# Gated attention plus feed-forward: when a native P V step may be begun in two halves

## The chip, the cores and the metric

The kernel runs on one core of one Trainium2 chip. The metric is the device time of one execution in microseconds (us). The kernel before was timed three times: 1029.58, 1030.44 and 1033.46 us, median 1030.44 us. The profile shown below is of one more execution.

## The reference, cut to what matters

Multi-query attention (32 heads of 16, one shared key and value head) and a feed-forward block with SiLU work on the same 2048 x 512 input; a sigmoid gate per row mixes their outputs.

```python
q = (x @ wq) in 32 heads of 16; k = x @ wk; v = x @ wv      # x: 2048 x 512
p = softmax(einsum("bhqd,bkd->bhqk", q, k) * 16 ** -0.5)
a = einsum("bhqk,bkd->bhqd", p, v) in 512 columns @ wo
b = silu(x @ w1) @ w2                                       # 512 -> 1792 -> 512
g = sigmoid((x * gate_w).sum(-1))
out = g * a + (1 - g) * b
```

## The kernel before, in words

**Work.** The queries are four chunks of 512 rows; the heads are taken eight at a time. So there are 16 rounds (chunk c, head group o). A round goes over the 2048 keys in 32 steps of 64 keys: 512 steps. A step has two halves j, each with four heads, and each half is one *score* on TensorE (PE; `scores(p)`, line 1225, eight matmuls into one of two `S` banks in PSUM) and one *exponential* on ScalarE (ACT; `exponential(p)`, line 1231). So p, the number of a score and of its exponential, runs from 0 to 1023, and step s has p = 2s and 2s + 1. A score of p needs the bank that exponential p - 2 has left. Both exponentials of a step write one buffer `P` (128 x 2048 float32). There are four such buffers (P_575 to P_578 in the order of instructions), and three more come when three chunks of the input are no longer needed (from about p = 280 on; they lie in the tile `xs`). Exponential 2s needs a buffer that no earlier step still uses.

**P V.** Each step's probabilities are then multiplied by the values (line 1262; `pv`), in one of two manners that the planner picks step by step. *In parts*: VectorE (DVE) takes the difference of P and its upper half as a float16 tile `L` (line 1237, two instructions a step; `L` buffers and two tiles `raw`), and PE makes a pass A on the upper halves and a pass B on `L`. *Native*: PE multiplies the float32 P itself, no DVE work. A native step is done whole (kind "W", eight matmuls of 512 columns, sixteen records in the trace) or, with `HALVES`, in two halves (kind "NM": N on the first 256 columns of each head, M on the others, eight matmuls of 256 columns each); other work may stand between N and M. P is released after M, W, or after A and both `L`.

**Feed-forward, projections.** Their matmuls (line 851) are cut into *passes* of eight matmuls. They are the filler: the planner puts them where PE has nothing more pressing. The hidden units go through a tanh on ACT (line 906) and two DVE instructions.

**Ends of rounds.** The accumulators `pv0`, `pv1` of a round are read by DVE (line 1151, two transposes) before the next round's first P V may start. So at the start of a round the exponentials run ahead into the free P buffers.

**Order.** All of this is ordered when the program is built, by a planner that lets a clock run for each of PE, ACT and DVE and takes for each engine the next piece of work (`advance`, `pe_next`, `act_next`, `dve_next`). On the chip each engine works down its list in that order, and waits where a result that it needs is not there. `pe_next` gathers candidates (ready time, price, kind): a score (price 0), P V (price 1 where the buffers are about to run out or the end is near, 3 for a step in parts or one already begun, 4 for a new native step), a pass (2 while the passes are behind their quota, else 5; 4.5 at the end of a round). Of those ready within 0.03 us of PE's clock it takes the cheapest, else the one that is ready first. `pv_next` offers a native step whole if it ends before the next score is due by the plan. Where it would not, but a half would, it offers "NM":

```python
fits = most if s not in left_of else most + HALF
if HALVES and r is not None and s not in left_of and max(r, now["PE"]) > most:
    fits, kind = most + HALF, "NM"
```

Of the kernel before, what the change touches and what calls it, by code (L numbers as in the profile page):

```python
# [33 lines left out]
BOW = 40 / 2.0 ** 18  # L34

DUE = 2.5
HALVES = True
PAIRS = 3
XUSE = "PPP "
GROUPS = (4, 3, 4, 3), (4, 3, 4, 3), (4, 3, 4, 3), (4, 4, 4, 2)  # L40
# [16 lines left out]
def kernel(  # L57
# [30 lines left out]
    x = x.rearrange("b s d -> (b s) d")  # L88
# [720 lines left out]
    def attention(ctx, pO, scale_of, t_scale, shifts, split_pieces, chores, q_todo, early, gates_, v_bank):  # L809
# [652 lines left out]
        exp_done, mm_done, how, left_of, low_done, pv_done, pv_free = {}, {}, {}, {}, {}, {}, {0: 0.0}  # L1462
# [57 lines left out]
        def pv_next(most):  # L1520

            best = None
            for s in range(head[0], min(head[0] + n_bufs[0], n_exp[0] // 2)):
                i, k = steps[s]
                if i != steps[head[0]][0] or k == NK - 1 and s != head[0]:
                    break
                r = pv_ready(s)
                ab = s in left_of and left_of[s] and left_of[s][0] in "AB"
# [3 lines that stand above are left out]
                else:  # L1532
                    kind = "W"
                if r is not None and (ab or max(r, now["PE"]) <= fits):
                    p = 1 if n_exp[0] - 2 * s >= 2 * n_bufs[0] + LAG - 8 or n_exp[0] >= 2 * len(steps) - SOON else 3 if ab else 4
                    new = (max(r, now["PE"] + 0.03), p, r, s, kind)
                    best = min(best or new, new)
                if s == head[0] and k == 0 and (s not in left_of or left_of[s] == list(how[s])):
                    break
            return best  # L1540
# [35 lines left out]
        def pe_next():  # L1576

            t, p = now["PE"], n_mm[0]
            cands = []
            if p < 2 * len(steps) and (p < 2 or p - 2 in exp_done) and placed[0] > steps[p // 2][1] * 64 // 512:  # L1580
                cands.append((exp_done[p - 2] if p > 1 else START, 0, "S", None))
            q = n_exp[0]
            end = max(now["ACT"], mm_done.get(q, 0.0)) + (p - q) * EXP
            x = pv_next(end - PASS_S - LATE - 2 * HALF + SLACK if p < 2 * len(steps) else 1e9)
            if x:
                cands.append((x[2], x[1], "P", x[3:]))
            if begin_:
                r = begin_[0][0]()
                if r is not None:
                    cands.append((r, begin_[0][1](), "R", None))  # L1590
            else:
                r = work.ready()
                if r is not None:
                    near = head[0] < len(steps) and steps[head[0]][1] >= NK - 2 and 0 < work.n - work.i <= KEEP
                    cands.append((r, 4.5 if near else 2 if work.passes < QUOTA * p + 3 * KD * len(early) - 30 - BOW * p * (2 * len(steps) - p) else 5, "F", None))
            ok = [x for x in cands if x[0] <= t + 0.03]
            return min(ok, key=lambda x: x[1]) if ok else min(cands, key=lambda x: x[0], default=None)

        def act_next():
# [60 lines left out]
        def on_dve(t, n):  # L1660
# [5 lines left out]
            return length  # L1666

        engines = {"PE": (pe_next, on_pe), "ACT": (act_next, on_act), "DVE": (dve_next, on_dve)}

        def advance():  # L1670
# [94 lines left out]
```

## Time and profile before

| | |
|---|---|
| median of three runs | 1030.44 us (1029.58 to 1033.46) |
| the profiled execution's own time | 1030.14 us |
| its span, first to last instruction | 1028.4 us |
| exponentials on ACT | 1024, the first begins at 25.7 us, the last at 1014.6 us |
| tanh instructions on ACT | 56 |
| busy shares on the page | PE 98%, ACT 96%, DVE 90% |
| P V steps before (of 512) | 245 in parts, 130 native whole, 131 native in halves, 6 at the end by code of their own |

The trace gives every instruction its engine, start and length. Two things have to be kept in mind. A matmul's record is longer than the time that it holds PE, since matmuls run into one another: what a piece of work costs on PE is read from its start to the start of what follows. And the record of an exponential is longer than the distance to the next one, so a small delay between two exponentials leaves no idle time in a view of waits; it too is read from start to start. In the time line, rows of one kind are merged: "x5" are five instructions.

### The profile page before, as it was taken

To read this page: it belongs to the slowest core of one execution; us is meant where nothing else is said; L and a number is where in the kernel's file an instruction comes from. 1 tells how busy PE (TensorE), PEld (TensorE's weight loads), DVE (VectorE), ACT (ScalarE), POOL (GpSimd) and SP (SyncE) were. 2 spreads that over 40 slices of the span, in tenths; PEclk is the share of its full clock that TensorE was granted. 3 is DMA by queue.
4 is the path that set the end of the run, shared out by engine and by line. 5 is a ranking of instruction groups with operands and counts; after the bars stand their busy time and mean duration, and the time that the engine had idled before them with its cause. 6 is when DMAs were issued, how large, how long until landed. Compare 5 with 4: busy or idle time off the path is not lost.

```text
span 1028.4 us, 69785 instructions
## 1 busy us (share of the span) xinstructions
PE 1006.5 (98%) x32760; PEld 616.2 (60%) x32760; DVE 924.5 (90%) x1199; ACT 992.3 (96%) x1108; POOL 60.0 (6%) x138
## 2 busy tenths in 40 slices
PE   8999999999999999999999999999999999999996
PEld 6456565666655656565656556566666556565563
DVE  7888978989999999999999999899998989999893
ACT  5999999999999999999999999999999999999994
POOL 4101101100000000000000000000000000000000
PEclk9999999999999999999999999999999999999999
DMA  5123322311010111101011010100110110101001
GB/s 208 48 87 85 82 59 60 76 45 25 10 42 18 48 33 25 30 5 32 19 24 41 24 46 15 35 20 15 47 27 17 43 39 10 36 10 19 5 4 47
DMA packets 28115, 40.14 MB, mean 39 GB/s; under 512 B 5689, under 2 KB 19370, under 8 KB 27818
## 3 DMA queue, kind: packets, MB, share of 16 engines
q0 software_dynamic: 10656, 15.73, 7.4%
q1 hardware_dynamic: 16442, 19.27, 5.9%
q8 instruction: 258, 4.23, 1.8%
q10 hardware_dynamic: 720, 0.59, 0.2%
q14 instruction: 39, 0.32, 0.1%
HBM read 19.98 MB, written 8.25 MB: 27 GB/s over the span
## 4 chain that ended last, share of the span: by engine, by line
PE 83%; ACT 10%; DVE 3%; issue 3%; DMA 1%; SPq 0%; ACTq 0%
PE pm L851 32%; PE pv L1262 28%; PE S L1225 20%; ACT P L1231 7%; ACT xs L1231 2%; DVE L L1237 1%; ACT e L906 1%; PE pv L1250 1%; DMA xn<-in_A_x_dram 1%; PE pt L339 0%; DVE xs L132 0%; DVE e L909 0%; PE pv L518 0%; PE pm L436 0%; PE S L1218 0%
## 5 line engine op out<-in xcount | busy, mean ns | idle before, releaser
L1231 ACT ACTIVATE P<-S 128x1024 f32<-128x1024 f32 x770 | 737.5, 1077 | 10.5 <-PE S L1225 5.5
L1225 PE MATMUL S<-qb,KT 50*32 50x512 f16 x8096 | 483.4, 379 | 5.7 <-ACT P L1231 1.8
L1225 PEld LDWEIGHTS <-KT 50*32 50x32 f16 x8096 | 206.1, 90 | 189.1 <-issue 100.0
L1237 DVE TENSOR_TENSOR L<-P 128x1024 f16<-128x1024 f32 x227 | 271.5, 1217 | 20.7 <-ACT P L1231 19.6
L851 PE MATMUL pm<-xs,w1s 64*32 64x512 f16 x5376 | 274.8, 375 | 1.1 <-DVE e L909 0.8
L851 PE MATMUL pm<-w2s,H 64*32 64x512 f16 x5376 | 273.8, 375 | 1.3 <-DVE e L909 0.8
L1262 PE MATMUL pv<-P,VF 64*32 64x256 f32 (+1 forms) x5056 | 267.5, 450 | 0.3
L1231 ACT ACTIVATE xs<-S 128x1024 f32<-128x1024 f32 x254 | 253.6, 1080 | 2.1 <-PE S L1225 0.9
L851 PEld LDWEIGHTS <-w1s 64*32 64x32 f16 x5376 | 126.5, 93 | 44.2 <-issue 8.4
L851 PEld LDWEIGHTS <-H 64*32 64x32 f16 x5376 | 125.3, 93 | 44.0 <-issue 4.3
L1237 DVE TENSOR_TENSOR raw<-P 128x1024 f16<-128x1024 f32 x109 | 131.1, 1218 | 2.3 <-ACT P L1231 2.0
L1262 PEld LDWEIGHTS pv<-P,VF 64*32 64x32 f32 x5056 | 112.1, 106 | 34.3 <-issue 3.3
L1237 DVE TENSOR_TENSOR L<-xs 128x1024 f16<-128x1024 f32 x90 | 108.0, 1218 | 3.9 <-ACT xs L1231 3.4
L1262 PEld LDWEIGHTS <-VP 64*32 64x32 f16 x3920 | 79.5, 92 | 36.0 <-issue 5.5
L851 PE MATMUL pm<-xs,wqs 64*32 64x512 f16 x1440 | 100.3, 375 | 0.1
L1262 PE MATMUL pv<-L,VP 64*32 64x512 f16 x1268 | 92.3, 375 | 0.3 <-DVE L L1237 0.2
L1262 PE MATMUL pv<-P,VP 64*32 64x512 bf16 x1344 | 81.9, 387 | 0.0
L1237 DVE TENSOR_TENSOR raw<-xs 128x1024 f16<-128x1024 f32 x64 | 76.9, 1217 | 2.4 <-ACT xs L1231 2.2
L851 PE MATMUL pm<-wo_s,O 64*32 64x512 f16 x1440 | 75.1, 375 | 0.6 <-issue 0.2
L918 POOL DMA_DIRECT2D H<-e x56 | 30.4, 542 | 729.4 <-DVE e L909 725.2
L1262 PE MATMUL pv<-xs,VF 64*32 64x256 f32 (+1 forms) x1216 | 62.5, 432 | 0.2 <-issue 0.2
L1262 PE MATMUL pv<-raw,VP 64*32 64x512 f16 x692 | 58.3, 375 | 0.0
(215 smaller groups left out, 710.5 us busy)
## 6 DMA issues: line engine op xcount, KB each, us to landing
H<-e POOLq DMA_DIRECT2D x56, 128.0 KB, 2.5
raw<-in_B_w_dram POOLq DMA_DIRECT2D x24, 256.0 KB, 3.3
qb<-qd SPq DMA_DIRECT2D x180, 32.0 KB
xn<-in_A_x_dram SPq DMA_DIRECT2D x8, 512.0 KB
out_dram<-acc SPq DMA_DIRECT2D x14, 256.0 KB
qd<-qx SPq DMA_DIRECT2D x13, 256.0 KB
raw<-in_A_wo_dram POOLq DMA_DIRECT2D x4, 256.0 KB, 3.1
qb<-sh SPq DMA_DIRECT2D x60, 2.0 KB
```

Source lines behind the costliest of these rows:

```text
L851: nc.tensor.matmul(self.bank[32 * m:32 * m + 32], l(i, rows, 32 * m), r(j, rows), start=first, stop=last)
L906: nc.scalar.activation(e, o.bank, AF.Tanh, scale=t_scale)
L918: nc.gpsimd.dma_start(H[:, 0], e)
L1225: nc.tensor.matmul(sc[32 * m:32 * m + 32, f], KT[b:b + 50, k0:k0 + 32], qtile[i][b:b + 50, m // 2, j], start=True, stop=True)
L1231: nc.scalar.activation(probs[s][:, 2 * j:2 * j + 2], banks.pop(p), AF.Exp, scale=scale_of(*rounds[steps[s][0]]))
L1237: nc.vector.tensor_tensor(lows[s, j], probs[s][:, js], upper(probs[s])[:, js], op=OP.subtract)
L1250: nc.tensor.matmul(pvs[i][h][32 * j:32 * j + 32, 256 * q:256 * q + 256], VF[r, NK - 2 * PAIRS + 2 * u + a], probs[s][r, j, 256 * a:256 * a ...
L1262: nc.tensor.matmul(pvs[i][h][32 * j:32 * j + 32, q], a[r], b[r, q], start=k == 0 and n != "B", stop=k == NK - 1 and n in "BMW")
```

## The change

Where `pe_next` has a new native step on offer that would be begun in halves, it now looks at the other candidates. P V has one candidate at a time, so these are the score and the pass (and the pieces of the beginning). If one of them is ready before PE's clock plus 0.2 us, the step in halves is struck from the list at that moment. It is offered again at the next decision, whole if it then fits. A half M of a step that has been begun is not held back, and price 1 makes no exception. The flag `HALVES` stays true; nothing is changed in what any instruction does.

```diff
-HALVES = True
+HALVES, GAP = True, 0.2
...
             ok = [x for x in cands if x[0] <= t + 0.03]
+            new = [x for x in ok if x[2] == "P" and x[3][1] == "NM" and x[3][0] not in left_of]
+            if new and min((x[0] for x in cands if x not in new), default=1e9) < t + GAP:
+                ok = [x for x in ok if x not in new]
+                cands = [x for x in cands if x not in new]
             return min(ok, key=lambda x: x[1]) if ok else min(cands, key=lambda x: x[0], default=None)
```

Every decision after the first one that differs is made from another state, so the order is dealt anew from there to the end. The counts of the first and only executed pass over the data, from the order of instructions: 244 steps in parts (245 before), 186 native whole (130), 76 native in halves (131). Scores, exponentials, passes and the last six steps are the same in number.

Three places on PE follow, where the prediction speaks of the order. `S_...` is a score, `pv0...<-P_...,VF` with 32x512 a native step done whole, with 32x256 a half of one, `<-P_...,VP` pass A and `<-L...,VP` pass B of a step in parts. "..." leaves out the rest of a piece's eight matmuls, their weight loads and the passes of line 851.

The first place, scores 30 to 32 of round 0, is where the two orders part. Before, the step in P_575 is begun in halves just ahead of score 30:

```order
L1262 MATMUL pv0_791<-P_575,VF_63 32x256
...
L1225 MATMUL S_1359<-qb0_83,KT_60 32x512
...
L1262 MATMUL pv1_792<-P_575,VF_63 32x256
...
L1225 MATMUL S_1377<-qb0_83,KT_60 32x512
...
L1262 MATMUL pv0_791<-P_576,VF_63 32x512
...
L1225 MATMUL S_1399<-qb0_83,KT_60 32x512
```

Now:

```order
L1225 MATMUL S_1348<-qb0_83,KT_60 32x512
...
L1262 MATMUL pv0_791<-P_575,VF_63 32x512
...
L1225 MATMUL S_1369<-qb0_83,KT_60 32x512
...
L1262 MATMUL pv0_791<-P_576,VF_63 32x256
...
L1225 MATMUL S_1400<-qb0_83,KT_60 32x512
```

The half ahead of score 30 is gone, the step in P_575 follows that score whole, and the next native step, whole before, is now the one in halves (its other half comes after score 33).

The second place is the start of round 2: exponential 136 is the first that needs a buffer back from this round. Before, the last P V of round 1 (`pv0_2593`) is the half behind score 132, and the first of round 2 (`pv0_4688`) stands ahead of score 137:

```order
L1262 MATMUL pv0_2593<-P_575,VF_63 32x256
...
L1225 MATMUL S_4559<-qb0_83,KT_60 32x512
...
L1262 MATMUL pv1_2594<-P_575,VF_63 32x256
...
L1225 MATMUL S_4677<-qb0_83,KT_60 32x512
...
L1262 MATMUL pv0_4688<-P_578,VF_63 32x512
...
L1225 MATMUL S_4700<-qb0_83,KT_60 32x512
```

Now (`pv0_4643` is round 2):

```order
L1225 MATMUL S_4527<-qb0_83,KT_60 32x512
...
L1225 MATMUL S_4561<-qb0_83,KT_60 32x512
...
L1262 MATMUL pv0_2593<-P_577,VF_63 32x512
...
L1225 MATMUL S_4632<-qb0_83,KT_60 32x512
...
L1262 MATMUL pv0_4643<-P_575,VF_63 32x512
```

The last P V of round 1 is a whole step behind score 133 (S_4561) in place of a half behind score 132, and the first of round 2 stands behind score 137 (S_4632), one score later than before.

The third place is score 222, whose exponential needs a buffer. Before, its buffer came free with a whole step behind score 218. Now the step that holds it, in P_575, is begun in halves ahead of score 223 and ended behind it:

```order
L1225 MATMUL S_7424<-qb1_84,KT_60 32x512
...
L1262 MATMUL pv0_6624<-P_575,VF_63 32x256
...
L1225 MATMUL S_7450<-qb1_84,KT_60 32x512
...
L1262 MATMUL pv1_6625<-P_575,VF_63 32x256
...
L1262 MATMUL pv0_6624<-P_577,VP_61 32x512
...
L1262 MATMUL pv0_6624<-P_576,VP_61 32x512
```

Score 222 is S_7424, score 223 is S_7450. Behind scores 219 to 222 stand eleven passes of line 851 ahead of that half.

## The prediction

> **What bounds the kernel now.** I read the page first, then ACT's exponentials by their starts, then the time line of PE around native steps, then the waits for P buffers.
>
> ```profile
> PE 1006.5 (98%) x32760; PEld 616.2 (60%) x32760; DVE 924.5 (90%) x1199; ACT 992.3 (96%) x1108; POOL 60.0 (6%) x138
> L1231 ACT ACTIVATE P<-S x770: 1014/1062/1278, 25.7 to 1014.6; 128x1024 f32<-128x1024 f32 x193
> L1231 ACT ACTIVATE xs<-S x254: 1014/1062/1293, 282.3 to 1012.6; 128x1024 f32<-128x1024 f32 x127
>   PE S L1225: 6.4, 20
>   PE pv L1262: 1.3, 4
> L906 ACT ACTIVATE e<-pm x56: 591/652/825, 79.3 to 942.6; 128x512 f32<-128x512 f32 x56
> 600.26 1.94 ACT L1231 ACTIVATE xs<-S 128x1024 f32<-128x1024 f32 x2
> 602.07 3.80 ACT L1231 ACTIVATE P<-S 128x1024 f32<-128x1024 f32 x4
> 605.68 0.67 ACT L906 ACTIVATE e<-pm 128x512 f32<-128x512 f32 x1
> 606.15 3.86 ACT L1231 ACTIVATE P<-S 128x1024 f32<-128x1024 f32 x4
> ```
>
> The first row is the page's busy times; both PE and ACT look full, so busy shares alone do not decide. The last four rows give ACT's own pace: four exponentials from 602.07 to 605.68, 0.903 us each, and a tanh holds it 0.47 us (605.68 to 606.15). From the first exponential's start to the last one's, 25.7 to 1014.6 us, are 988.9 us; 1023 x 0.903 + 56 x 0.477 make 950.5. So ACT lies still for some **38 us**, and this is all that another order can change between the ends: 25.7 us ahead and 13.8 behind hold no choice that the change touches. The view of what ACT waits for names only 6.4 us for scores and 1.3 us for P V, since neighbouring exponentials overlap by about 0.15 us in the records: a delay below that shows as no idle time. Read from start to start, 119 exponentials come over 0.1 us late, 29 us in all.
>
> PE's own work is less than ACT's. Its prices stand in this stretch of round 0:
>
> ```profile
> 53.66 0.42 PE L1262 MATMUL pv<-P,VP 64*32 64x512 bf16 x8
> 53.89 0.41 PE L1225 MATMUL S<-qb,KT 50*32 50x512 f16 x8
> 54.10 0.41 PE L1262 MATMUL pv<-L,VP 64*32 64x512 f16 x8
> 54.32 0.41 PE L851 MATMUL pm<-xs,wqs 64*32 64x512 f16 x8
> 54.54 0.63 PE L1262 MATMUL pv<-P,VF 64*32 64x256 f32 x16
> 54.97 0.41 PE L1225 MATMUL S<-qb,KT 50*32 50x512 f16 x8
> 55.19 0.63 PE L1262 MATMUL pv<-P,VF 64*32 64x256 f32 x16
> 55.62 0.41 PE L1225 MATMUL S<-qb,KT 50*32 50x512 f16 x8
> 55.84 1.05 PE L1262 MATMUL pv<-P,VF 64*32 64x512 f32 x16
> 56.70 0.41 PE L1225 MATMUL S<-qb,KT 50*32 50x512 f16 x8
> 52.70 4.69 ACT L1231 ACTIVATE P<-S 128x1024 f32<-128x1024 f32 x5
> ```
>
> From start to next start: pass A 0.23, a score 0.22, pass B and a feed-forward pass 0.22 each, a half 0.43, a whole native step 0.86. A score with three passes (0.87) or with a pass and a half (0.87) fits into an exponential's 0.903; a score with a whole step (1.08) does not, and lives on the exponential that is ahead. With these prices the instructions from score 0 on hold PE 934 us of the 989. So PE has some 55 us of slack, and ACT is late only where PE's work comes in lumps, where a buffer is not back, or where the plan's clock and the chip differ.
>
> **The change part by part.**
>
> *Halves become whole steps.* 131 split steps become 76, so 55 are done at one piece. Rows 54.54 to 56.70 price that: 0.43 + 0.43 against 0.86, **0** in PE's time, and the same weight loads overlapped. Bounds from the nearest rows: another half, 300.60 to 301.06 below, takes 0.46, so 110 halves fewer could free 110 x 0.03 = 3.3 us of PE; nothing excludes a whole step that costs 0.01 more (0.6 us). Nearly all halves read 0.43, so I take 0.
>
> ```profile
> 300.60 0.63 PE L1262 MATMUL pv<-P,VF 64*32 64x256 f32 x16
> 301.06 0.41 PE L1225 MATMUL S<-qb,KT 50*32 50x512 f16 x8
> ```
>
> [...]
>
> *One step in parts becomes native* (245 to 244): 0.86 in place of 0.23 + 0.22, so +0.41 us on PE, and two differences on DVE less. It lies in PE's slack; bounds 0 and 0.41, I take **+0.2**.
>
> *What stands ahead of each score.* A score can be late only by what PE does ahead of it. I sorted the delays of before by the last piece ahead of the score (170 behind a half, 119 behind a whole step, 478 behind a pass, 123 behind A, 102 behind B), first and last of the two that matter here:
>
> ```profile
> 32.69 1.09 PE L1262 MATMUL pv<-P,VF 64*32 64x512 f32 x16
> 34.08 0.59 PE L1225 MATMUL S<-qb,KT 50*32 50x512 f16 x9 [0.30 <-issue]
> 989.63 1.05 PE L1262 MATMUL pv<-P,VF 64*32 64x512 f32 x16
> 990.49 0.41 PE L1225 MATMUL S<-qb,KT 50*32 50x512 f16 x8
> 1000.51 0.59 PE L1262 MATMUL pv<-P,VF 64*32 64x256 f32 x8
> 1000.86 0.39 PE L1225 MATMUL S<-qb,KT 50*32 50x512 f16 x4
> ```
>
> The first half is that of 54.54. The exponentials start 0.054 us late on average behind a half, 0.068 behind a whole step, 0.028 behind a pass, 0.013 behind A, 0.021 behind B. In the new order there are 77 scores behind a half, 167 behind a whole step, 517 behind a pass, 119 behind A and 111 behind B. That is -5.0 us for the halves, +3.3 for the whole steps, +1.1 for the passes and +0.1 for A and B: **-0.5 us**, bounds -5.0 (whole steps and passes stay as good as they are now placed) and +4.5 (the halves that go are those that cost nothing). Sorted instead by how much work lies between two scores, the same delays priced for the new order give +0.3, so I stay near nothing. The mean is the right choice between the ends, since the planner's rule strikes halves by its own clock and not by what the chip shows.
>
> *P buffers.* What the change adds is waiting: a native step is put off, passes go first, and with it the buffer that it holds comes back later. Queued behind a missing buffer is the exponential on ACT, and behind it both S banks, so PE's next scores. Up to p = 280, with four buffers, this is what happens now:
>
> ```profile
> 153.32 5.60 ACT L1231 ACTIVATE P<-S 128x1024 f32<-128x1024 f32 x6
> 159.43 4.73 ACT L1231 ACTIVATE P<-S 128x1024 f32<-128x1024 f32 x5 [0.51 <-PE pv L1262]
> 105.01 2.86 ACT L1231 ACTIVATE P<-S 128x1024 f32<-128x1024 f32 x3
> 108.10 1.02 ACT L1231 ACTIVATE P<-S 128x1024 f32<-128x1024 f32 x1 [0.23 <-PE pv L1262]
> 221.98 1.03 ACT L1231 ACTIVATE P<-S 128x1024 f32<-128x1024 f32 x1
> 223.35 1.02 ACT L1231 ACTIVATE P<-S 128x1024 f32<-128x1024 f32 x1 [0.34 <-PE pv L1262]
> 271.98 1.94 ACT L1231 ACTIVATE P<-S 128x1024 f32<-128x1024 f32 x2
> 274.14 1.02 ACT L1231 ACTIVATE P<-S 128x1024 f32<-128x1024 f32 x1 [0.21 <-PE pv L1262]
> 156.04 1.31 DVE L1151 STREAM_TRANSPOSE T<-pv 128x512 f32<-128x512 f32 x2
> 158.05 0.41 PE L1225 MATMUL S<-qb,KT 50*32 50x512 f16 x8 [0.28 <-ACT P L1231]
> 158.26 1.05 PE L1262 MATMUL pv<-P,VF 64*32 64x512 f32 x16
> ```
>
> The four rows with a wait are exponentials 136, 84, 202 and 254. Start to start they are late by 6.11 - 6 x 0.903 = 0.69, 3.09 - 2.71 = 0.38, 1.37 - 0.90 = 0.47 and 2.16 - 1.81 = 0.35 us. In the orders I looked up for each p up to 280 where the last P V on its buffer stands. Before, five stand behind the score of p itself: those four, and p = 38. Now p = 84, 202 and 254 have their buffer back a score earlier (-1.2 us), 38 stays, and two are worse. *Exponential 136*: the new round's first P V moves behind score 137. On the chip it already starts at 158.26, 0.9 after DVE ended its transposes (156.04 + 1.31 = 157.35), because score 137 (158.05) waited. The last P V of round 1 now comes about 1.5 us of PE work later (a score, two passes and a whole native step more), which eats the 0.9. I put it at **+0.4**, bounds 0 and +1.5. *Exponential 222*: its buffer comes back with the half behind score 223, a score, a pass and a half (0.87) later than in the cases just priced: 0.38 + 0.87 to 0.47 + 0.87, **+1.2**, and at least 0.4. Together **+0.4**, bounds -0.8 and +1.9. With five buffers and more no exponential waits for P V now, and I put 0 there.
>
> *Sum*: 0 + 0.2 - 0.5 + 0.4 = **+0.1 us** on the profiled execution's own 1030.14 (span 1028.4 and 1.7 around it). It lies 0.3 below the median of the runs, so the forecast against them is 1030.5. As the second sorting and the lumps of the new order (two scores with over 1.9 us of work to the next, where before none has over 1.6) lean to more, I say **1031 us**.
>
> **The rivals.**
>
> *More is lost at the buffers (slower).* The guard makes no exception where buffers run out. Over all 15 changes of round the last P V of a round stands 6 scores later in sum (67 behind the round's last score against 61). With five to seven buffers there is no wait for P V in the view of before, which speaks against it; it decides from the point where the release falls a score behind the score of the exponential that needs it, as at 222. Six scores at 0.9 are 5.4 us, with the sum **1036.5 us**.
>
> *Scores really come free (faster).* Of the delays behind halves, 9.2 us now, those go that the guard strikes, and whole steps cost nothing more because they are put where they fit: -5.0 in place of -0.5, the four buffer waits go as well (-0.8), **1025 us**. Against it: 1.08 us for a score and a whole step is 0.18 over ACT's pace, and 167 of them come in place of 119.
>
> *The cut itself costs PE time.* If halves cost as the row at 300.60, 3.3 us of PE come free, and as PE sets the pace only in part, about half of it: **1029 us**. The rows at 54.54 and 55.19 speak against it. [...]
>
> *It does nothing that it says.* Only score and pass are looked at, not a step in parts, and 53 of the 76 remaining first halves still have a score right behind them (109 of 131 before), as a score may come due after 0.2 us and before the half's 0.43 ends. Then only the dealing anew is left: 1030.4, inside the forecast.
>
> **How the numbers follow.** Any new deal moves the delays: the root of the sum of their squares is 3.3 us now, an estimate of how far one order strays from the mean of its like; the difference of two orders strays 1.4 times as far, 4.6 us. So the likeliest, **1031 us**, has a chance of 0.64; in it are 0.04 for the third rival and 0.10 for the fourth, which end in the same band; more lost at the buffers 0.22; scores freed 0.14. 0.5% (5.2 us), about what a measurement of this kernel can tell from no change, is at 1025.3 and 1035.6. The range reaches to the faster rival and just beyond the slower one, **1025.5 to 1037 us**. Faster by over 0.5%: 0.13. Within: 0.66. Slower: 0.21.
>
> **What would show it.** Right: ACT's exponentials from the first start to the last again some 989 us, with waits of ACT for P V near 136 and 222 and none at 84, 202, 254; whole native steps at 0.86 and halves at 0.43 from start to start; waits of ACT for scores between 4 and 9 us. The step on scores is wrong if ACT's waits for scores move by more than 3 us; the step on buffers if ACT's waits for P V pass 3 us or lie behind p = 280. A span between the first and last exponential below 984 or over 994 would make the forecast wrong.

## The result and the profile after

The changed kernel takes **1023.27 us** (median of 6 runs, 1022.0 to 1026.59) beside 1032.08 for the kernel before on the same chip: a ratio of **0.9925** (95% interval 0.9906 to 0.9943). It is faster by 0.75%, where 1031.0 and no measurable change were forecast. The time lies below the predicted range. On another chip the same kernel took 1023.65 us, at a ratio of 0.9908 (0.9884 to 0.9931).

These are rows of the page of the changed kernel (busy us, share of the span, instructions; the queue's row has packets, MB and share) and of its view of line 1231, the exponentials.

```profile
span 1021.7 us, 68003 instructions
PE 1001.4 (98%) x31880; PEld 599.6 (59%) x31880; DVE 921.4 (90%) x1197; ACT 988.3 (97%) x1108; POOL 59.9 (6%) x138
q8 instruction: 251, 4.11, 1.7%
...
L1231 ACT ACTIVATE P<-S x770: 1015/1084/1263, 25.6 to 1006.7; 128x1024 f32<-128x1024 f32 x193
L1231 ACT ACTIVATE xs<-S x254: 1017/1108/1221, 277.8 to 1008.5; 128x1024 f32<-128x1024 f32 x127
  PE S L1225: 5.3, 16
  PE pv L1262: 2.9, 3
```

The exponentials still begin at 25.6 us, but the last one starts at 1008.5 in place of 1014.6. The stretch between is 983.0 us in place of 988.9. Their own pace needs the same 950.5, so the time that ACT loses fell from 38.4 to 32.5 us. Another 0.6 us came off the end, behind the last exponential. Nearly all of the gain lies in the last quarter: in the last 255 exponentials the loss is 5.8 us in place of 11.5.

The profile's own list of waits tells little of this. ACT waits 5.3 us for scores (6.4 before) and 2.9 for P V (1.3 before), which is a gain of 1.1 and a loss of 1.6. What shrank are delays of 0.1 to 0.3 us from start to start, most of which show as no idle time: there were 93 of them with 16.1 us in sum, and there are 63 with 10.3. Longer ones make 13.0 us in both kernels.

PE's matmul records fell by 880, from 32760 to 31880. That is 16 matmuls for each of 55 steps, and as many weight loads. The queue that brings the instructions moved 251 packets in place of these:

```profile
q8 instruction: 258, 4.23, 1.8%
```

That is the row of the kernel before. 4.23 MB over 258 packets are 16.4 KB each.

### The profile page after: what moved, and what is told of

It is laid out like the page before. It is cut to its first block, busy times and chain, and to the rows that moved or that the text cites. A ratio compares the mean times of both kernels' runs of the same rounds, so it can differ in the third digit from the quotient of the medians.

```text
span 1021.7 us, 68003 instructions
## 1 busy us (share of the span) xinstructions
PE 1001.4 (98%) x31880; PEld 599.6 (59%) x31880; DVE 921.4 (90%) x1197; ACT 988.3 (97%) x1108; POOL 59.9 (6%) x138
## 3 DMA queue, kind: packets, MB, share of 16 engines
q8 instruction: 251, 4.11, 1.7%
## 4 chain that ended last, share of the span: by engine, by line
PE 68%; ACT 16%; issue 8%; DVE 6%; DMA 1%; SPq 0%; ACTq 0%; DVEq 0%; POOLq 0%
PE pm L851 27%; PE pv L1262 23%; PE S L1225 17%; ACT P L1231 12%; ACT xs L1231 4%; DVE L L1237 2%; ACT e L906 1%; DVE e L909 1%; DMA wqr<-in_A_wq_dram 1%; DVE raw L1237 0%; DMA H<-e 0%; DVE xs L132 0%; PE pt L339 0%; PE pv L1250 0%; DVE acc L830 0%
## 5 line engine op out<-in xcount | busy, mean ns | idle before, releaser
L1225 PE MATMUL S<-qb,KT 50*32 50x512 f16 x8096 | 456.0, 379 | 4.3 <-ACT P L1231 2.1
L1225 PEld LDWEIGHTS <-KT 50*32 50x32 f16 x8096 | 203.1, 89 | 212.1 <-issue 118.8
L1237 DVE TENSOR_TENSOR L<-P 128x1024 f16<-128x1024 f32 x231 | 276.0, 1218 | 16.6 <-ACT P L1231 16.3
L851 PE MATMUL pm<-xs,w1s 64*32 64x512 f16 x5376 | 269.6, 375 | 1.0 <-DVE e L909 0.5
L851 PE MATMUL pm<-w2s,H 64*32 64x512 f16 x5376 | 267.5, 375 | 2.1 <-DVE e L909 1.1
L1262 PE MATMUL pv<-P,VF 64*32 64x512 f32 (+1 forms) x4400 | 246.5, 493 | 0.1
L851 PEld LDWEIGHTS <-H 64*32 64x32 f16 x5376 | 121.2, 93 | 45.8 <-issue 5.2
L1262 PEld LDWEIGHTS pv<-P,VF 64*32 64x32 f32 x4400 | 92.7, 106 | 24.8 <-issue 2.5
L1262 PEld LDWEIGHTS <-VP 64*32 64x32 f16 x3904 | 74.1, 92 | 35.3 <-issue 4.9
L851 PE MATMUL pm<-wo_s,O 64*32 64x512 f16 x1440 | 68.6, 375 | 0.1
L1262 PE MATMUL pv<-xs,VF 64*32 64x512 f32 (+1 forms) x1008 | 57.9, 494 | 0.1
```

Of the source, the lines that this page charges most:

```text
L851: nc.tensor.matmul(self.bank[32 * m:32 * m + 32], l(i, rows, 32 * m), r(j, rows), start=first, stop=last)
L1225: nc.tensor.matmul(sc[32 * m:32 * m + 32, f], KT[b:b + 50, k0:k0 + 32], qtile[i][b:b + 50, m // 2, j], start=True, stop=True)
L1237: nc.vector.tensor_tensor(lows[s, j], probs[s][:, js], upper(probs[s])[:, js], op=OP.subtract)
L1262: nc.tensor.matmul(pvs[i][h][32 * j:32 * j + 32, q], a[r], b[r, q], start=k == 0 and n != "B", stop=k == NK - 1 and n in "BMW")
```

## The experiments

A ratio is that to the kernel before on the same chip. Diffs are against the changed kernel where nothing else is said, and "cut" means that a native step is issued as two halves.

### Is a cut free?

**All steps cut**, the order untouched, both halves back to back. 246 steps are cut in place of 76.

```diff
-            pv(s, n)
+            for part in ("NM" if n == "W" and steps[s][1] and s < ends_at else n):
+                pv(s, part)
```

> The changed kernel with its order untouched; every whole native step (but the first of each round and the last six) is issued as its two halves back to back, 246 steps cut in place of 76. Theory 'the cut is free, only the place of a half counts' (rows of before: 0.43 + 0.43 = 0.86): the time of the changed kernel, 1023 us, ratio to before 0.9925 within 0.002. Theory 'the cut itself costs PE time' (0.03 us a half, as one row of before had it): 340 halves more by 0.03 is 10 us of PE, half of it on the path, 1028 us or more, ratio 0.997 or more.

Measured: 1061.1 us, 1.0282 (1.0261 to 1.0302). Against the changed kernel 170 more cuts cost 38 us, 0.22 each. The price of nothing was wrong. Yet at the place from which the prediction read it, it still reads as it did. First the time line of PE in the changed kernel, then the same step in this one:

```profile
54.70 1.05 PE L1262 MATMUL pv<-P,VF 64*32 64x512 f32 x16
55.56 0.41 PE L1225 MATMUL S<-qb,KT 50*32 50x512 f16 x8
```

```profile
55.10 1.06 PE L1262 MATMUL pv<-P,VF 64*32 64x256 f32 x32
55.96 0.41 PE L1225 MATMUL S<-qb,KT 50*32 50x512 f16 x8
```

From the step's start to the score's it is 0.86 us, whole or cut. So the price is not paid in the step. It shows in the view of groups (busy us, mean ns of one, idle time ahead and what ended it) as time in which the weight loads waited for nothing that the profile shows, the changed kernel first:

```profile
L851 PEld LDWEIGHTS <-w1s 64*32 64x32 f16 x5376 | 123.6, 93 | 43.2 <-issue 8.0
L851 PEld LDWEIGHTS <-H 64*32 64x32 f16 x5376 | 121.2, 93 | 45.8 <-issue 5.2
L1262 PEld LDWEIGHTS pv<-P,VF 64*32 64x32 f32 x4400 | 92.7, 106 | 24.8 <-issue 2.5
L1225 PEld LDWEIGHTS <-KT 50*32 50x32 f16 x8096 | 203.1, 89 | 212.1 <-issue 118.8 <-DVE qb L582 0.6 <-ACT qb L581 0.4
```

```profile
L851 PEld LDWEIGHTS <-w1s 64*32 64x32 f16 x5376 | 133.5, 93 | 54.9 <-issue 17.9
L851 PEld LDWEIGHTS <-H 64*32 64x32 f16 x5376 | 130.1, 93 | 54.8 <-issue 14.4
L1262 PEld LDWEIGHTS pv<-P,VF 64*32 64x32 f32 x6624 | 145.0, 106 | 51.9 <-issue 9.2
L1225 PEld LDWEIGHTS <-KT 50*32 50x32 f16 x8096 | 207.0, 90 | 141.9 <-issue 61.7 <-DVE qb L582 0.6 <-ACT qb L581 0.4
```

The feed-forward passes of line 851 weren't touched, and their loads wait 32.3 us in place of 13.2 in these two groups. That suggested that PE runs dry of instructions. It is no proof: in the last row, the largest such group, the loads of the scores went the other way, from 118.8 us to 61.7, so this kind of idle time is not all want of instructions. A native float32 matmul stands in the records as two matmuls and two weight loads, so a half is 32 instructions in 0.43 us, 13.4 ns each, and so are a score or a pass with 16 in 0.22. A whole step is 32 in 0.86, so by this reading it is the one piece in which the supply could run ahead.

**The same number of cuts as before.** 53 whole steps are cut in this kernel, so that 129 are, beside 131 in the kernel before. In a second one, timed together with the changed kernel, 48 others are, 124 in all.

```diff
+            for part in ("NM" if n == "W" and steps[s][1] and s < ends_at and s % 10 in (1, 4, 7) else n):
+                pv(s, part)
```

> The changed kernel with its order untouched; 53 of its whole steps (those whose number ends in 1, 4 or 7 and that were whole) are issued as their two halves back to back, so that 129 are cut, as many as in the kernel before (131). If the price of cutting is what the change saves, and the order is worth nothing: 53 x 0.17 to 0.22 us more than the changed kernel's 1023, 1032 to 1035, the time of before. If the order is worth the gain and the cut only costs where all are cut: 1023 to 1026. In between, the part above 1023 over 9 is the share of the price.

> The changed kernel itself, on the chip of the next three: a ratio of 0.991 to 0.994 to before. It is there so that the price of the next one is a difference on one chip.

> The changed kernel with its order untouched, 48 of its whole steps issued as two halves back to back (other steps than the 53 of the earlier run: numbers that end in 0, 3 or 6), 124 cut in all. Price of the cut as the whole gain: 48 x 0.16 (8.8 us over 55) = +7.5, 1031. Order as the whole gain: +0 to 1.5. As in the run with 53 cuts: +2.5 to 5.

Measured: with 53 cuts 1029.01 us, 0.995 (0.9935 to 0.9964). With 48 cuts 1031.18 us, 0.9977 (0.9961 to 0.9994), and the changed kernel on that chip 1023.65. The 48 cuts cost 7.5 us, **0.157 us each**; the slowest run of the changed kernel there (1024.17) is well below the fastest with the cuts (1028.78). Little of it is in the step: halves back to back hold PE 0.864 us in the median and 0.880 in the mean, whole steps in the changed kernel's run beside it 0.860 and 0.868. The 53 cost 5.7 us by the medians but only 0.25% by the ratios, 0.05 to 0.11 each, on different chips. At 0.157 the 55 cuts that the change leaves out are worth 8.6 us, which is the gain; at the low end they are worth a third of it.

Since the order is the changed kernel's own, one sees where a cut is paid for. In the run with 48 cuts ACT loses 39.8 us in place of 32.7 in the changed kernel's run beside it. Behind passes it is 13.7 in place of 9.9, behind whole or newly cut steps 15.7 in place of 14.0, behind A 2.3 in place of 1.2. More than half of the added delay is met by scores that stand behind a pass, not behind the cut step. The run with 53 cuts shows less of this: of some 5 us more than in the changed kernel, 0.5 to 1.9 stand behind passes and 2.3 to 4.3 behind halves and whole steps. The bounds come from the two traces of the changed kernel beside which it can be set, and from how the pieces are told apart.

### Is it the supply of instructions?

**The same order, moved within the packets.** Ten of the 15 warming transposes at the start give way to 64 short matmuls, so that PE's program is 108 instructions longer ahead of the first score, and all that follows lies 108 further on in packets of some 254 (63,760 matmuls and loads of PE in the changed kernel over its 251 packets, an estimate).

```diff
-            for _ in range(15):
+            for _ in range(5):
                 nc.tensor.transpose(warm[:, 0:128], ident, ident)
+            for _ in range(64):
+                nc.tensor.matmul(warm[:, 0:8], ident.bitcast(F16)[:, 0:128], ident.bitcast(F16)[:, 0:8], start=True, stop=True)
```

> The changed kernel, its order untouched after the start; 10 of the 15 warming transposes at 1.4 us are replaced by 64 short f16 matmuls, so that PE's program is 108 instructions longer ahead of the first score, and each later piece lies 108 of 256 further on in the packets of 16 KB that bring the instructions. Supply: the stalls near a packet move: the waits of the exponentials that start near 93.0, 105.2, 135.1, 362.6 and 526.2 us fall below 0.2 us and others of their size come in other places; the total within 1019 to 1028. Order (a piece is late because of what stands ahead of it, whatever packet it lies in): the same waits at the same places, total within 1022 to 1024.5.

Measured: 1023.1 us, 0.9922 (0.9902 to 0.9942). The total is the same, and the stalls named are gone. Here is one of them, in the time line of the changed kernel:

```profile
133.41 0.40 PE L851 MATMUL pm<-w2s,H 64*32 64x512 f16 x5
134.42 0.39 PE L851 MATMUL pm<-w2s,H 64*32 64x512 f16 x3 [0.62 <-issue]
134.42 0.09 PEld L851 LDWEIGHTS <-H 64*32 64x32 f16 x2 [1.04 <-issue]
134.43 0.60 PE L1225 MATMUL S<-qb,KT 50*32 50x512 f16 x8
135.14 1.02 ACT L1231 ACTIVATE P<-S 128x1024 f32<-128x1024 f32 x1 [0.72 <-PE S L1225]
```

Five of the eight matmuls of a pass have gone out, then PE has nothing for a microsecond, and goes on in the middle of the pass. Nothing in the program waits there. The score behind it is late, and exponential 110 with it. The same place in the shifted kernel:

```profile
132.39 0.53 PE L1227 MATMUL S<-qb,KT 50*32 50x512 f16 x8
132.61 0.74 PE L1264 MATMUL pv<-P,VF 64*32 64x256 f32 x16
133.04 0.52 PE L853 MATMUL pm<-w2s,H 64*32 64x512 f16 x8
133.26 0.52 PE L1227 MATMUL S<-qb,KT 50*32 50x512 f16 x8
132.13 2.86 ACT L1233 ACTIVATE P<-S 128x1024 f32<-128x1024 f32 x3
```

No gap and no wait. All five exponentials named in the expectation lost their delay: 68, 80, 110, 345 and 516 were late by 0.68, 0.61, 0.84, 0.57 and 0.50 us, and are now within 0.02 of their pace. Others took their place (104, 188, 201, 277 and 495, with 0.40 to 0.64 us). Delays that a buffer or the order sets stayed, as the 1.55 us of exponential 136. In both kernels most such stalls end 1.0 to 1.3 us before the next packet of the instruction queue begins (of gaps over 0.42 us, 5 of 8 and 9 of 10). For the stall above that packet lies in the window from 135.4 to 135.6 us, where the view of the queues has one row:

```profile
q8 instruction: 1, 0.02, 27.3%
```

That the shift moved these stalls is not shown, though. The second run of the changed kernel, on another chip, has the same order and the same packets, and there exponentials 68, 80 and 110 are on their pace too, and 345 and 516 late by 0.31 and 0.23 us. The place of the stall in that run:

```profile
131.60 0.62 PE L1262 MATMUL pv<-P,VF 64*32 64x256 f32 x16
132.04 0.41 PE L851 MATMUL pm<-w2s,H 64*32 64x512 f16 x8
132.25 0.41 PE L1225 MATMUL S<-qb,KT 50*32 50x512 f16 x8
```

A packet begins there at 133.16 us, 1.12 us behind the start of this pass (1.04 behind the end of the stall above), and PE doesn't stand. Such stalls come and go between two executions of one program. What the traces do show is where they stand when they come, and that the order alone does not make them.

**What of the whole lies near the packets.** For each trace I took the time in which PE did less than its matmuls' own prices from start to start (0.2155 us for eight in f16, 0.43 for a half, 0.86 for a whole step, from 40 us to 10 us ahead of the last exponential), apart for the time 0.9 to 2.1 us ahead of an instruction packet and for the rest:

```
kernel                 cuts   near a packet   elsewhere   sum    ACT late
no halves                 0       18.5          43.1      61.6     36.6
limit 0.4                25       16.8          33.9      50.7     28.9
rule, dealt anew         70       18.5          34.2      52.7     36.5
changed                  76       20.8          29.7      50.5     32.5
changed, again           76       22.5          28.2      50.7     32.7
changed, shifted         76       17.3          34.5      51.8     33.1
score alone              97       21.1          28.7      49.8     32.9
pass alone               97       18.5          32.0      50.5     33.4
urgent steps exempt     112       26.1          27.3      53.5     37.2
before, dealt anew      124       31.4          25.7      57.1     38.5
changed, 48 cuts        124       25.1          31.8      56.9     39.8
changed, 53 cuts        129       25.4          30.0      55.4     37.6
before                  131       24.2          31.9      56.1     38.4
all cut                 246       51.0          33.7      84.7     67.7
```

The six kernels with 70 to 97 cuts lose 19.8 us near the packets and 31.2 elsewhere, in the mean; the five with 112 to 131 lose 26.4 and 29.3. With all cut it is 51.0 near the packets. So more cuts cost mainly there, though for one pair (changed again and 48 cuts) only 2.6 of the 6.2 us fall into that window. Three things weaken this. The windows are 30% of the time, so 15 of the 19.8 us and 17 of the 26.4 would lie in them by chance. The three runs of the changed kernel's order differ by 5 us among themselves. And the two kernels with joined steps of the last section (67 cuts) are not in the table: on a grid of 0.1 us, which gives the other rows within about 1 us, they lose 22 and 26 us near a packet and 42 and 34 elsewhere.

A narrower count goes with the cuts in all kernels. Take, between 40 and 990 us, the gaps of over 0.42 us from one start on PE, of a matmul or a load, to the next that ended on nothing the profile shows, and 1.0 to 1.3 us ahead of a packet. There are 1 and 0 of them without halves and with the limit at 0.4, 5 and 4 in the joined kernels, 5 in the rule dealt anew, 5, 9 and 9 in the three runs of the changed order, 8 and 6 with 97 cuts, 9 to 17 with 112 to 131, and 57 with all cut. In sum they are 3.9 to 5.2 us long in the changed order, 6.8 before and 33.5 with all cut. This ties long stalls at packets to the cuts, and gives them some 2 to 3 us of the change's 6 on ACT.

**More weight loads in whole steps**, meant to raise the number of instructions without a matmul.

```diff
+                    if n == "W" and s < ends_at:
+                        for _ in range(4):
+                            nc.tensor.ldweights(VP[r, k], tile_position=(64 * h, 32 * j))
```

> The changed kernel with its order untouched; after each of the eight matmuls of a whole step (189 whole steps) PE gets four more loads of a 64x32 f16 weight into the tile that the matmul used, 32 more instructions a step and 6,048 in all. The next matmul loads its own weights over them, so the result is the same and no matmul is added. Supply (PE runs dry of instructions, since a cut step hands it 64 in the 0.86 us in which a whole one hands it 32): the cut of 170 steps cost 38 us, 0.22 a step, so 189 x 0.22 gives 1023 + 42 = 1065; at least 1045, with PE idle for nothing that the profile shows, as in the run in which all steps were cut. Array (the cut costs because a half has its own start and end in the array): no matmul is added, the loads overlap, 1023 to 1028. If the whole steps themselves grow from 0.86 us, the loads cost array time and the run tells the two apart only by where the time lies.

Measured: 1168.14 us, 1.1333 (1.1308 to 1.1358). Neither forecast of the time was met, and it doesn't decide between the two. The trace holds 5,952 added loads in 186 steps, so one costs (1168.14 - 1023.27) / 5952 = 24 ns. The time line has steps that grew, as this one of 1.21 us:

```profile
53.63 1.30 PE L1263 MATMUL pv<-P,VF 64*32 64x512 f32 x16
54.84 0.54 PE L1226 MATMUL S<-qb,KT 50*32 50x512 f16 x8
```

But most did not. The median from a whole step's start to the next piece's is 0.86 us as before (mean 0.98, beside 0.87 in the changed kernel), and it is the score behind that holds PE 0.50 us in the median in place of 0.22:

```profile
502.53 1.26 PE L1263 MATMUL pv<-P,VF 64*32 64x512 f32 x16
503.39 0.87 PE L1226 MATMUL S<-qb,KT 50*32 50x512 f16 x8
503.89 0.42 PE L437 MATMUL pm<-e,kab 64*32 64x512 f16 x2
```

So here too most of a step's added time falls on the pieces behind it. Whether for want of instructions or because the score's own loads stand behind the 32 added ones, this run can't tell.

**Fewer instructions for the same work**: scores with 64 weight columns in place of 32.

```diff
-            for m in range(4):
+            for u in range(2):
                 for f in range(2):
                     b = 64 * f
-                    k0 = kt * 64 + 32 * (m % 2)
-                    nc.tensor.matmul(sc[32 * m:32 * m + 32, f], KT[b:b + 50, k0:k0 + 32], qtile[i][b:b + 50, m // 2, j], start=True, stop=True)
+                    nc.tensor.matmul(sc[64 * u:64 * u + 64, f], KT[b:b + 50, kt * 64:kt * 64 + 64], qtile[i][b:b + 50, u, j], start=True, stop=True)
```

> The changed kernel with its order untouched; each score's eight matmuls with 32 weight columns are four with 64, on the same operands, so that the result is the same and 8,096 instructions of PE are left out (of some 64,000). Supply alone: at the price of a cut's 32 instructions (0.17 to 0.22 us) up to 40 us, but no more than the stalls near a packet hold (PE's shortfall 1 to 2 us ahead of a packet is 18.6 us in the changed kernel, some 8 of it the mean of other times): 1012 to 1018. If a change of the tile's shape costs PE time, twice a score: 1,012 x 2 changes, at 0.02 us each already +40: above 1050.

Measured: 1241.93 us, 1.2015 (1.1998 to 1.2032). What the wider scores cost hides whatever the 8,096 instructions would have freed: 218.7 us, and with all of it put down to the 2 x 1012 changes between 64 columns and 32, 0.108 us each, an estimate. In the time line the score now holds PE 0.34 us in place of 0.22, and the pass ahead of the next score 0.35 in place of 0.22, so the time is lost on both sides of a score:

```profile
60.81 0.41 PE L1224 MATMUL S<-qb,KT 50*64 50x512 f16 x4
61.15 0.66 PE L1261 MATMUL pv<-P,VF 64*32 64x256 f32 x16
61.60 0.42 PE L851 MATMUL pm<-xs,wqs 64*32 64x512 f16 x8
61.95 0.41 PE L1224 MATMUL S<-qb,KT 50*64 50x512 f16 x4
```

### Which part of the rule, and is it luck?

The rule was split into its parts: only scores looked at, only passes looked at, and a step that the planner prices as urgent left out of it.

```diff
-            if new and min((x[0] for x in cands if x not in new), default=1e9) < t + GAP:
+            if new and min((x[0] for x in cands if x[2] == "S"), default=1e9) < t + GAP:
```

> The guard looks at the score alone, not at the pass. Theory 'the guard strikes the halves that make a score late': about the changed kernel's time, ratio 0.992 to 0.995, the delay behind first halves falls from 0.065 us each to about 0.025. Theory 'the gain comes from letting passes go first': no gain, ratio 0.998 to 1.002. Theory 'a fresh deal of the order, by luck': anything within 0.996 to 1.004, without a link to the halves.

> The guard looks at the pass alone, not at the score. Theory 'the guard strikes the halves that make a score late': little gain, ratio 0.997 to 1.001, since 80 first halves still stand ahead of a score. Theory 'letting passes go first': the changed kernel's time, 0.992 to 0.995.

> The guard makes an exception where the step's price is 1, that is where the P buffers run out. In the changed kernel's profile two exponentials wait 1.55 and 1.44 us for a buffer (136 and 222). If these waits are a cost of the guard that can be had back: they fall to 0.7 and nothing, 2 us less, 1021 us, ratio 0.990 to 0.992. If the halves that come back (112 in place of 76) make scores late as those of before did: 36 x 0.065 is 2.3 us lost again, 1023 to 1026 us, ratio 0.993 to 0.996.

Measured: score alone 1024.95 us, 0.9921 (0.9902 to 0.994); pass alone 1025.66, 0.9935 (0.9915 to 0.9956); urgent steps exempt 1032.44, 0.9995 (0.9976 to 1.0014). The first two have 97 cuts each and nearly the whole gain, so it hangs on neither part. The third has 112 and none of it, where a gain was expected either way. It is 7 us slower than the first two on the same chip; its 15 cuts more are 2.4 us at 0.157, so the count of cuts alone doesn't account for it.

Then both kernels were dealt anew, by one of the planner's constants:

```diff
-EXP, EXP_DONE, TANH, TANH_DONE, LOW = 0.905, 1.10, 0.48, 0.67, 1.15
+EXP, EXP_DONE, TANH, TANH_DONE, LOW = 0.905, 1.101, 0.48, 0.67, 1.15
```

> The kernel before, without the rule; one of the planner's constants (how long after its start an exponential is done) is 1.101 in place of 1.10, which deals the order anew: 145 whole steps, 124 in halves, 245 in parts (before: 131 in halves). Supply: 7 fewer cuts, 0.17 each: 1030 to 1032. Luck of the order (the gain of the change is one draw of many such orders): anywhere from 1022 to 1035, and then two draws that differ by 8 us say nothing of the rule.

> The changed kernel with the planner's constant 1.101 in place of 1.10, which deals the order anew with the rule in it: 204 whole steps, 70 in halves, 232 in parts. If the rule is worth the gain: 1020 to 1026, against 1030.1 for the same constant without the rule. If the gain was the luck of one draw: as likely above 1027 as below.

Measured: without the rule 1030.12 us, 0.9993 (0.9976 to 1.001); with it 1029.84, 0.9956 (0.994 to 0.9972). The medians are of different chips, so the ratios count. The rule is worth 0.37% in this deal (by the two intervals, give or take 0.23) and 0.75% in the other. The 1020 to 1026 expected with the rule were missed. The gain doesn't vanish with a new deal, and its size depends on it.

### Why not fewer still?

> The changed kernel with no step in halves at all (265 whole steps, none of 76 cut; the planner then cannot begin a native step in the gap ahead of something that is due). Supply: 2,432 fewer instructions for PE; at the price per cut of the run with all cut (0.17 to 0.22 us) 13 to 17 us less than the changed kernel's 1023, at most part of it lost to the coarser order: below 1020. Order (the gain came from the order alone, halves being useful where nothing is due): whole steps in place of halves make scores late, 0.076 us each by the whole steps' mean: 76 x (0.076 - 0.02) = +4, and steps delayed: 1026 to 1035.

> The changed kernel with the limit at 0.4 in place of 0.2 us: 246 whole steps, 25 in halves, 235 in parts. By the price of cuts alone, 51 fewer: 51 x 0.17 = 9 us less, 1014. With the coarser order's price, read from the run without halves (11.7 us above the changed kernel although it has 76 fewer cuts, so some 24 us for 76 steps that lost the choice, 0.32 each): 51 x (0.32 - 0.17) = +8, 1031. If the price lies in the last few halves only, in between: 1020 to 1026.

Measured: no halves 1034.82 us, 1.003 (1.0014 to 1.0045); the limit at 0.4, with 25 cuts, 1027.37, 0.9941 (0.9928 to 0.9953). The price of a cut alone would have given some 1010 and 1014. With the limit at 0.4 ACT loses least of all, 28.9 us, but PE has work left at the end: 19.0 us pass from the last exponential's start to the end of the span, in place of 13.2, and without halves 20.7. There passes of the feed-forward stand behind the last score. The time line of PE without halves:

```profile
1016.07 2.77 PE L851 MATMUL pm<-w2s,H 64*32 64x512 f16 x48
1018.77 1.98 PE L1719 MATMUL S<-qx,O 128*128 128x512 f32 x4
1020.59 2.75 PE L855 MATMUL S<-w2s,H 128*128 128x512 f16 x12
```

**What a half is good for.** In the kernel before, 64 cut steps have one score and nothing else between their halves. They were joined, the rest of the order left alone: once the whole step ahead of that score, once behind it (67 cuts are left in both). The diff is against the kernel before; `"N"` becomes `"M"` for the second.

```diff
-            pv(s, n)
+            if not early or s not in JOIN or n not in "NM":
+                pv(s, n)
+            elif n == "N":
+                pv(s, "W")
```

> The kernel before, its order untouched but for 64 of its 131 cut steps, those with one score and nothing else between the halves: they are issued whole, ahead of that score (67 cut are left, 2,048 instructions of PE fewer). Price of the cut: 64 x 0.05 to 0.16 = 3 to 10 us less, 1022 to 1029. If the cut costs nothing and halves only serve the scores: each such score is 0.43 us later, and up to that each is added where PE was late already: 1032 to 1045.

> As the last, but the whole step stands behind the score, which is issued 0.43 us earlier in PE's order. Price of the cut: 3 to 10 us less, 1022 to 1029. If the cut costs nothing: PE stands idle until the score's bank comes free, up to 0.43 us for each of 64 where PE was early: 1032 to 1050. If the score before the halves and the one ahead of them are both late already, both runs gain alike, and the order between the halves is worth nothing.

Measured: whole step first 1034.41 us, 1.002 (1.0001 to 1.0039); score first 1031.77, 0.9969 (0.995 to 0.9989). 64 cuts fewer should free 10 us at 0.157, and only 2 to 3 came with the score first. With the whole step first, the 64 exponentials of those scores are late by 19.5 us in sum, where it was 4.1. With the score first they are late by 0.8, but the next ones by 8.6 in place of 2.6. The list of ACT's waits shows the first:

```profile
ACT P L1232 <- PE S L1226: 10.7, 35, 0.7
```

By the price of 0.157 us a half beside a score is thus worth about what it costs. The two runs don't exclude the other reading, that a cut costs less in the order of before.

## Why the prediction was wrong

*What bounds the kernel.* That ACT loses 38 us between its first and last exponential, and that the change can act only there, held: 5.9 us of the 6.7 by which the profiled spans differ came out of it. That PE has 55 us of slack held as a number: the shortfall of PE in the table is as long (56.1 us before). But it is no reserve from which time lost on PE could be met: where the shortfall grows with the cuts, ACT's lateness grows too (changed again and 48 cuts: 6.2 us more on PE, 7.1 on ACT).

*Halves become whole steps: 0.* **This is the step that failed.** The working, "0.43 + 0.43 against 0.86", is right at the rows quoted and still reads so in the kernel with all steps cut. But a row in an undisturbed place can't show a price that is paid at another place. Measured in the changed kernel's own order it is 0.157 us a cut for 48 of them (0.05 to 0.11 for 53, 0.22 for 170), so 8.6 us for 55 by the one pair timed on one chip, and from 2.7 up by the other. What the runs showed in place of nothing is thus a price that falls for the most part on the pieces behind the step; by what way is argued, not shown. The bound of 3.3 us was too small as well: it came from one half that read 0.46.

*One step in parts: +0.2.* No run tells it apart from the rest.

*What stands ahead of each score: -0.5.* **This failed too, in part for the same cause.** The sentence was that "the mean is the right choice between the ends, since the planner's rule strikes halves by its own clock". Only the whole steps kept their mean, 0.076 us a score (9.1 us for 120, then 12.9 for 169, sorted as in the matmul order). Behind a half it fell from 0.054 to 0.023 (9.4 us for 173, then 1.8 for 79), behind a pass from 0.028 to 0.021 (13.6, then 11.1). Together with A and B the classes gave -7.2 us. The means were no property of the piece ahead: the run with 48 cuts returns 3.8 us to the class behind passes without moving one of them. Sorting delays by what stands just ahead can't price a cost that comes some pieces later. And behind halves more went than the mean allowed (7.6 us in place of 5.0), so the halves that were struck may have been dearer than the rest; no run tells this apart.

*P buffers: +0.4.* The mechanism was right, one size was off. ACT's time line after has the two waits that were named, at 136 and 222, beside one of 0.15 us at 38, which was to stay:

```profile
160.76 1.94 ACT L1231 ACTIVATE P<-S 128x1024 f32<-128x1024 f32 x2 [1.43 <-PE pv L1262]
...
245.52 1.94 ACT L1231 ACTIVATE P<-S 128x1024 f32<-128x1024 f32 x2 [1.32 <-PE pv L1262]
```

Exponentials 84 and 254 lost their delay, 202 kept 0.11 us. Start to start 222 is late by 1.44 us, against some 1.2 forecast. 136 went from 0.70 to 1.55, +0.85 where +0.4 was taken and +1.5 was the bound. The sum is about +1.2 in place of +0.4.

*The rivals.* More lost at the buffers did not come: no such wait lies behind p = 280. "Scores really come free" gave nearly the time (1025), and by the wrong way: it left whole steps as they were and let delays behind halves go because these were struck where a score is due. But two rules with 97 cuts each, one looking at scores alone and one at passes alone, gain alike. "The cut itself costs PE time" came nearest to what the added cuts showed, with 1029 us and a chance of 0.04; but its price was read off the one half at 300.60, in the step, where little of it is.

*What would show it.* Of the signs named, the span between the exponentials below 984 (983.0) marked the forecast as wrong. The sign on ACT's waits for scores, 4 to 9 us, held at 5.3 while the delays below it moved by 6 us: a list of idle times was the wrong place to look.

*What stays open.* How much of the gain is the price of the cuts and how much the deal of the order: between a third and all of it by the runs with 53 and with 48 cuts, a fresh deal gave half of the gain, and 64 cuts fewer in the order of before gave 2 to 3 us at best. That the price is the supply of instructions is argued: the long stalls stand at packets and their number goes with the cuts, which at the dose of the change gives 2 to 3 us, but no run changed the supply alone. For the rest the account rests on the means of the table, and part of the gain may be that the halves left out were those that made scores late.

## What to carry to other kernels

Price a split by a run in which the order stays and only the split is added, since its cost may be paid several pieces later; a clean stretch of the time line shows only that the piece itself is not longer. Where an engine issues without pause, count its instructions beside its busy time, and look in the groups for idle time that nothing ended. Before a stall that has gone is put down to an edit, look whether it stands in a second execution of the same kernel. A finer cut is worth its price only where something due goes into the gap it opens; struck everywhere, the work that no longer fits is left for the end.

## What the runs showed of the chip that was not expected

- PE's instructions come in packets of 16.4 KB (4.11 MB in 251 of the instruction queue q8). Their number goes with PE's matmuls and loads: 219 packets for 55,664 with the wide scores, 251 for 63,760 in the changed kernel, 272 for 69,200 with all steps cut. So a packet holds some 254 of them, some 64 bytes for each, an estimate from these counts. Pieces run at 13.4 to 13.5 ns an instruction (a half, a score, a pass) or 27 (a whole step).
- PE can stand for up to a microsecond in the middle of a piece (until 134.42 us above), and most such stalls end 1.0 to 1.3 us before the next packet begins (5 of 8 in the changed kernel, 9 of 10 in the shifted one). They are not the same in two executions of one program: of the five delays named in the run with the shift, a second execution without it had three not at all and two by half.
- An added 64x32 f16 weight load between float32 matmuls cost 24 ns in the total. The median whole step with 32 of them still took 0.86 us; the score behind it took 0.50 in place of 0.22.
- Scores of 64 weight columns among pieces of 32 cost 218.7 us; by the 2,024 changes from one to the other that is 0.108 us each, an estimate. The score held PE 0.34 us in place of 0.22, the pass ahead of it 0.35 in place of 0.22.
